# Recurrent attention and a routed expert layer on one core: state sums before routing, an earlier and smaller first list, one gather of late rows, index lists on VectorE

## The chip, the core and the metric

The kernel runs on one core of a Trainium2 chip. The metric is the time of one execution on the device, in microseconds (us); the kernel before was timed in 3 runs. One further execution was recorded by the hardware profiler, and all rows of a trace come from such an execution. Engine names: PE is TensorE's matmul, PEld its weight load, DVE is VectorE, ACT is ScalarE, POOL is GpSimd, SP is the engine that issues most transfers. Each engine works through its own instructions strictly in order and waits on the others by semaphores.

## The reference

```python
for t in range(S):                       # attention: 4 batches, 8 heads, 768 steps, width 40
    m_new = np.maximum(f_gate[:, :, t] + m, i_gate[:, :, t])
    f_stab = np.exp(f_gate[:, :, t] + m - m_new)
    i_stab = np.exp(i_gate[:, :, t] - m_new)
    C = f_stab * C + i_stab * outer(v_t, k_t)
    n = f_stab * n + i_stab * k_t
    y_t = sigmoid(o_t) * (C @ q_t) / max(abs(n . q_t), 1)
x = y as 3072 rows of 320
g_idx, g_w = argmax and softmax weight of x @ w_group            # 4 groups
e_idx, e_w = argmax and softmax weight of x @ w_expert[g_idx]    # 4 experts in each
out[row] = g_w * e_w * (relu(x[row] @ w1[g, e]) @ w2[g, e])      # 320 -> 1024 -> 320
```

Each of the 3072 rows goes to one of 16 experts. With the inputs of this case the fullest expert has 321 rows in the end, 267 after five of the six time chunks and 222 after four (counted with the reference).

## The kernel before

**Attention.** The 768 steps are cut into 6 chunks of 128, and a chunk of one batch is a unit: 24 units, number 4c + b, worked off in order of time by `unit(u)` (L958 to L1001) and, from unit 20 on, by the hand-written `last_units` (L1028 to L1144). All instructions are issued in the order in which this Python code calls them. For one unit PE does the scores (L199, tile `sp`), the products with the values (L281, `acc`), the new state (L248, `st`), the product with the state of earlier chunks (L229, `acc` of the next unit) and the transposes of the finished rows (L319, `tp`). POOL multiplies the state by its decay (L255, `Cflat`), the rows by their denominators (L301, `x`) and cuts the mask triangle (L158, `ab`); ACT takes the exponentials (L190). DVE forms the denominators and gated rows (L286 to L296), scales `acc` (L238), multiplies scores by the mask (L204, `pt`, two instructions) and adds the new state (L266, two instructions). `st` and the two `acc` banks have one buffer each, so a unit's state product waits until the state sum of the unit before has read `st`.

**Routing.** When four units of a chunk are done, `chunk_logits` (L348) and the generator `route` (L364) find each row's expert and its place in that expert's list, in 18 short steps that `go_on` deals out over the next units: six ahead of `scores` in three of four units (L959, L970). `mark` (L481) then builds one-hot matrices, and PE adds them to the lists (L501, `listed` L505).

**First expert.** After three chunks `first_experts` (L550) chooses the expert with most rows. Its list is drawn by `select` (L509) in `last_units` when five chunks are listed (L1102); up to 256 rows are gathered early, and the first layer runs after the last unit in `early_expert` (L707, PE L720 first layer, L735 to L737 second). The rows of that expert which come later are collected by another way: `late_marks` and `late_rows` (L522, L529) multiply the rows of the last units, still in SBUF, by selection matrices on PE, and `late_gather` (L1013) fetches the rest. They run as a second narrow pass of the same expert, `expert((0, 1), ...)` (L1336).

**All experts.** `expert` (L857) runs experts 1 to 15 one after the other, first layer at L780, second at L825 to L833; number r has CAPS[r] slots, so 6 and 7 have the same width (224), as have 11 to 14 (160). From number 6 on they are narrow: DVE adds two halves (`hs`, L888) before each relu. Weights are split into a high and a low part, by ACT (L750) and DVE (L754). At the start of expert r, `load_ix(r + 2)` (L665) draws the list of expert r + 2 with `select` on POOL: a product `lsel` on POOL (L511), its sum `lsum` on DVE (L513), two index writes on POOL (L519, L520). POOL also issues all gathers (L636) and scatters (L640), and after some experts waits until its scatters have drained (L849).

```python
        select(r, top[:, r, :] if r < NPICK else rt["sel"][:, r, :], nc.gpsimd)
...
        ahead, behind = STEPS.get(u) or ((6, 0), (2, 0), (6, 0), (6, 1))[u % B]
...
        go_on(ahead)
```

Of the kernel before, what the change touches and what calls it, by code (L numbers as in the profile page):

```python
# [18 lines left out]
P = 128  # L19
# [25 lines left out]
SIDE = (B, B, B, B, B - 1)  # L45
# [4 lines left out]
HAND = 20  # L50
# [12 lines left out]
def lstm_moe(ctx: ExitStack, tc: tile.TileContext, gates, qkT, nat, wcat, w1, w2, cst, out):  # L63
# [7 lines left out]
    peek = dram.tile([1, 2], F32, name="peek")  # L71
# [22 lines left out]
    late_f = const.tile([P, NEARLY], F32, name="late_f")  # L94
# [24 lines left out]
    abs_ = [ap_.tile([P, H, P], F32, name=f"ab{i}") for i in range(4)]  # L119
    nts = [ap_.tile([P, NTW + DM + WIN], F32, name=f"nt{i}") for i in range(4)]  # L120
    ps_s = att.enter_context(tc.tile_pool(name="ps_s", bufs=3, space=PSUM))
# [177 lines left out]
    def rows(u, e=None):  # L299
        x = wk.tile([P, ROW], F32, name="x", bufs=3) if u < HAND else mxp.tile([P, ROW], F32, name="xg", bufs=8)  # L300
        (e or nc.gpsimd).tensor_tensor(x[:, 0:DM].rearrange("p (h d) -> p h d", d=D), st_[u]["sr"],  # L301
                                       bc(st_[u]["den"].unsqueeze(2), (P, H, D)), op=ALU.mult)
        st_[u]["x"] = x

    def store_rows(u):
# [4 lines left out]
        if c == NCH - 1:  # L310
            no_order("early", ins, "store")
# [27 lines left out]
    def logits(u):  # L339
        c, b = divmod(u, B)  # L340
        if c < NCH - 1 and b < SIDE[c]:
            return chunk_logits(SIDE[c]) if b == SIDE[c] - 1 else None
        if b == 0:
            rt["bank"] = ps_1.tile([P, LG + B * 20], F32, name="lg")
        for k, (x, w) in enumerate(terms(b)):
            mm(rt["bank"][:, LG + b * 20:LG + (b + 1) * 20], x, w[:, 0:20], start=(k == 0), stop=(k == 2))

    def chunk_logits(n):  # L348
        bank = rt["bank"] = ps_1.tile([P, LT + P], F32, name="lg")
        for k in range(3):  # L350
            for b in range(n):
                x, w = terms(b)[k]
                mm(bank[32 * b:32 * (b + 1), LT - P:LT], w, x, start=(k == 0), stop=(k == 2))
        nc.scalar.copy(lgT[0:32 * n, :], bank[0:32 * n, LT - P:LT])

    def turned_logits(c):
        bank, n = rt["bank"], SIDE[c]
        lv = bank[:, LT:LT + 32 * n]
        nc.tensor.transpose(out=lv, in_=lgT[0:32 * n, :], identity=ident[0:32 * n, 0:32 * n])
        return route(c, 0, n, bank, lv.rearrange("p (b e) -> p b e", e=32)[:, :, 0:20], n < B)  # L360
# [3 lines left out]
    def route(c, b0, b1, bank, lv=None, ahead=False):  # L364

        n = b1 - b0
        cur, nxt = ohsum[rt.setdefault("n", 0) % 2], ohsum[(rt["n"] + 1) % 2]
        rt["n"] += 1
        if lv is None:
            lv = bank[:, LG + b0 * 20:LG + b1 * 20].rearrange("p (b e) -> p b e", e=20)  # L370
# [27 lines left out]
        def sums():  # L398
            ohs = post.tile([P, NE], BF16, name="ohs")
            with nc.allow_low_precision("whole numbers up to 4"):  # L400
                nc.vector.tensor_reduce(ohs, oh.rearrange("p b e -> p e b"), axis=AX.X, op=ALU.add)
            nc.vector.tensor_tensor(nxt, cur, ohs, op=ALU.add)

        if ahead:
            sums()
        rk = bank[:, b0 * NE:b1 * NE].rearrange("p (b e) -> p b e", b=n)
# [5 lines left out]
        if b1 == B:  # L412
            cnt = bank[:, B * NE:B * NE + NE]
            mm(cnt, ones_b, cur, start=True, stop=False)
            for b in range(n):
                mm(cnt, ones_b, oh[:, b, :], start=False, stop=(b == n - 1))
        yield
        if b1 == B:
# [1060 lines left out]
```

## Time and profile before

| | us |
|---|---|
| median of 3 runs | 452.38 |
| lowest and highest run | 449.66, 454.95 |
| the profiled execution, its own time | 456.12 |
| span of its trace, first to last instruction | 454.5 |
| PE busy | 406.7 (89%) |
| DVE busy | 336.9 (74%) |
| ACT busy | 261.7 (58%) |
| POOL busy | 186.1 (41%) |
| mean granted PE clock | 0.939 of full speed |

The span starts and ends with the first and last instruction; 1.6 us of the execution lie around it. A busy share is a mean over stages with different limits: an engine at 74% can be what everyone waits for in one stage and idle in another.

### The profile page before, as it was taken

To read this page: it belongs to the slowest core of one execution; us is meant where nothing else is said; L and a number is where in the kernel's file an instruction comes from. 1 tells how busy PE (TensorE), PEld (TensorE's weight loads), DVE (VectorE), ACT (ScalarE), POOL (GpSimd) and SP (SyncE) were. 2 spreads that over 40 slices of the span, in tenths; PEclk is the share of its full clock that TensorE was granted. 3 is DMA by queue.
4 is the path that set the end of the run, shared out by engine and by line. 5 is a ranking of instruction groups with operands and counts; after the bars stand their busy time and mean duration, and the time that the engine had idled before them with its cause. 6 is when DMAs were issued, how large, how long until landed. Compare 5 with 4: busy or idle time off the path is not lost.

```text
span 454.5 us, 9459 instructions
## 1 busy us (share of the span) xinstructions
PE 406.7 (89%) x3369; PEld 377.9 (83%) x3369; DVE 336.9 (74%) x841; ACT 261.7 (58%) x621; POOL 186.1 (41%) x227
## 2 busy tenths in 40 slices
PE   8799779687877986789999999999799999998995
PEld 5688768577867775789999999999799998897994
DVE  5776685777676997768576756676688997997993
ACT  3486464555543643404455646656567886886783
POOL 6576346354544111106363152452343334664221
PEclk9889898989988999569999999999899999999899
DMA  6999878776765742701758465756466777776400
GB/s 183 310 304 303 260 213 265 218 220 210 205 207 181 262 181 61 274 17 43 272 195 321 162 205 170 259 187 234 178 211 222 239 257 266 241 260 265 149 16 11
DMA packets 22469, 93.59 MB, mean 206 GB/s; under 512 B 3746, under 2 KB 7801, under 8 KB 18836
## 3 DMA queue, kind: packets, MB, share of 16 engines
q1 hardware_dynamic: 18180, 78.64, 52.3%
q0 software_dynamic: 3920, 13.95, 9.2%
q8 instruction: 28, 0.46, 0.4%
q10 hardware_dynamic: 320, 0.37, 0.4%
q14 instruction: 21, 0.17, 0.2%
HBM read 83.41 MB, written 10.23 MB: 206 GB/s over the span
## 4 chain that ended last, share of the span: by engine, by line
PE 51%; issue 18%; DVE 13%; POOL 10%; ACT 4%; DMA 1%; POOLq 1%; SPq 0%; ACTq 0%; DVEq 0%
PE psh L780 13%; PE acc L229 5%; POOL out_dram L640 4%; PE po L825 4%; PE po L826 4%; PE po L827 4%; PE acc L281 3%; DVE pt L204 2%; PE sp L199 2%; PE psh L720 2%; PE tp L319 2%; PE st L248 2%; POOL ab L158 2%; PE psh L800 2%; POOL xg L636 2%
## 5 line engine op out<-in xcount | busy, mean ns | idle before, releaser
L780 PE MATMUL psh<-xhl,w1h 128*128 128x320 f32 (+4 forms) x336 | 87.7, 322 | 5.7 <-DVE hs L888 5.5
L640 POOL DMA_INDIRECT out_dram<-y,ix x34 | 43.3, 1275 | 108.8 <-ACT y L839 86.7
L780 PEld LDWEIGHTS psh<-xhl,w1h 128*128 128x128 f32 x336 | 57.4, 190 | 7.5 <-DVE hs L888 6.5
L825 PE MATMUL po<-w2h,hh 128*128 128x320 f32 (+1 forms) x184 | 58.5, 318 | 0.0
L754 DVE TENSOR_TENSOR w2l<-w2s,w2h 128x640 fp32r<-128x640 f32 x64 | 53.0, 845 | 6.0 <-ACT w2h L750 5.3
L826 PE MATMUL po<-w2l,hh 128*128 128x320 f32 (+1 forms) x184 | 57.0, 310 | 0.0
L827 PE MATMUL po<-w2h,hh 128*128 128x320 f32 (+1 forms) x184 | 56.9, 309 | 0.0
L190 ACT ACTIVATE ab<-ab,bcol 128x128 f32<-128x128 f32 x176 | 53.8, 389 | 4.3 <-POOL ab L158 3.8
L281 PE MATMUL acc<-nt,pt 128*128 128x128 f32 (+1 forms) x384 | 49.7, 283 | 5.6 <-ACT nt L155 3.2
L281 PEld LDWEIGHTS acc<-nt,pt 128*128 128x128 f32 x384 | 46.2, 196 | 9.0 <-ACT nt L155 3.4
L636 POOL DMA_INDIRECT xg<-x_d,ix x34 | 38.5, 1133 | 29.4 <-DVE lf L1023 15.4
L780 PE MATMUL psh<-xhl,w1l 128*128 128x160 f32 (+6 forms) x256 | 49.0, 273 | 0.0
L780 PE MATMUL psh<-xhl,wsk 128*128 128x320 f32 (+4 forms) x168 | 46.5, 315 | 0.9 <-DVE wsk L754 0.9
L750 ACT CAST w2h<-w2s 128x640 fp32r<-128x640 f32 x64 | 44.8, 723 | 0.0
L780 PEld LDWEIGHTS psh<-xhl,w1l 128*128 128x128 f32 x256 | 43.8, 190 | 0.5
L321 ACT COPY xT<-tp 128x256 f32<-128x256 f32 x24 | 8.9, 372 | 58.5 <-PE tp L319 34.2
L754 DVE TENSOR_TENSOR w1l<-w1s,w1h 128x1024 fp32r<-128x1024 f32 x32 | 38.9, 1220 | 3.7 <-ACT w1h L750 3.6
L204 DVE TENSOR_TENSOR pt<-sp,ab 128x512 f32<-128x512 f32 x48 | 31.1, 684 | 10.0 <-PE sp L199 8.5
L825 PEld LDWEIGHTS po<-w2h,hh 128*128 128x128 f32 (+1 forms) x184 | 34.4, 187 | 0.6
L826 PEld LDWEIGHTS po<-w2l,hh 128*128 128x128 f32 (+1 forms) x184 | 34.3, 186 | 0.0
L827 PEld LDWEIGHTS po<-w2h,hh 128*128 128x128 f32 (+1 forms) x184 | 34.2, 186 | 0.0
L750 ACT CAST w1h<-w1s 128x1024 fp32r<-128x1024 f32 x32 | 33.5, 1049 | 0.0
(221 smaller groups left out, 908.3 us busy)
## 6 DMA issues: line engine op xcount, KB each, us to landing
w1s<-in_w_dram SPq DMA_DIRECT2D x12, 1536.0 KB
w2s<-in_w_dram SPq DMA_DIRECT2D x13, 1280.0 KB
nt<-in_nat_dram SPq DMA_DIRECT2D x24, 484.0 KB
ab<-a_d SPq DMA_DIRECT2D x22, 512.0 KB
qk<-in_qkT_dram SPq DMA_DIRECT2D x48, 160.0 KB
x_d<-x SPq DMA_DIRECT2D x20, 192.0 KB
w1s<-in_w_dram SPq DMA_DIRECT2D x4, 768.0 KB
w1s<-in_w_dram POOLq DMA_DIRECT2D x2, 1536.0 KB, 7.3
```

The source lines that it names most:

```text
L190: nc.scalar.activation(ab[:, j, :], ab[:, j, :], AF.Exp, bias=bcol[:, c, b * H + j:b * H + j + 1])
L204: nc.vector.tensor_tensor(pt, t["pm"][hh], t["ab"][:, 4 * hh:4 * hh + 4, :], op=ALU.mult)
L229: mm(acc[:, 2 * pr:2 * pr + 2, 0:CW], t["qk"][:, 1, pr, :], Cflat[:, o:o + 2 * CW].rearrange("p (r e) -> p r e", r=2), start=(pr == 0), st ...
L281: mm(o, t["pm"][j % 2][:, j // 2, :], v, start=(c == 0 and n == 0), stop=(n == H - 1), skip_group_check=True)
L636: return nc.gpsimd.indirect_dma_start(out=o, out_offset=None, in_=src, in_offset=bass.IndirectOffsetOnAxis(ap=idx, axis=0))
L640: return nc.gpsimd.indirect_dma_start(out=out, out_offset=bass.IndirectOffsetOnAxis(ap=idx, axis=0), in_=y, in_offset=None, bounds_check=N ...
L750: nc.scalar.copy(t[names[0]][:, dst], src[r][:, s])
L754: nc.vector.tensor_tensor(o, src[r][rows, s], h.bitcast(F32), op=ALU.subtract)
L780: mm(ps[:, g, 0:n_], w[:, s], x, start=(n == 0), stop=(n == len(todo) - 1))
L825: mm(po[0:m], hh[:, f, t], w2h[:, s], start=st0, stop=False)
L826: mm(po[0:m], hh[:, f, t], w2l[:, s], start=False, stop=False)
L827: mm(po[0:m], hh[:, f, tl], w2h[:, s], start=False, stop=sp0)
```

## The change

Six things move. (1) In `unit`, the state sum (`state2`) comes before the masks, and the routing steps are dealt two by two: ahead of the scaling of `acc`, ahead of the masks, behind them. (2) Units 20 and 21 go through `unit` like the others; the four units of a chunk are always routed together. (3) The first expert's list is drawn in unit 21 from four chunks (16 units) in place of five; expert 0's weights are split in units 21 to 23, with the low parts on POOL. (4) The eight steps of its first layer are dealt among the last transposes, logits and routing; the second layer among the last lists. (5) The selection products of late rows go; when the lists are complete one gather, on POOL, fetches all late rows. (6) `select` runs on DVE alone, and the lists of experts 3 to 15 are drawn at the start of experts 1 to 7, two at a time from number 2.

```diff
     def unit(u):
-        ahead, behind = STEPS.get(u) or ((6, 0), (2, 0), (6, 0), (6, 1))[u % B]
+        one, two, three = STEPS.get(u) or ((2, 2, 1), (0, 0, 0), (2, 2, 2), (2, 2, 2))[u % B]
...
+        go_on(one)
         run(carried2, u)
         listed()
-        go_on(ahead)
         scores(u + 1)
...
         values(u)
+        run(state2, u)
+        go_on(two)
+        if u == NU - 3:
+            rt["early"] = select(top[:, 0, :], nc.vector)
+            xgs[0] = load_x(EARLY, rt["early"], True)
         masked(u + 1, 0)
         masked(u + 1, 1)
         store_rows(u - 1)
-        run(state2, u)
...
-        go_on(behind)
+        go_on(three)
...
+def early_first(W, ws):          # the loop of early_expert, one step f a yield
+        for f in range(NF):
...
+            if g:
+                relu(ps, f - 1)
+            yield
...
-    def casts(r):
+    def casts(r, e=None):
...
-                nc.vector.tensor_tensor(o, src[r][rows, s], h.bitcast(F32), op=ALU.subtract)
+                (e or nc.vector).tensor_tensor(o, src[r][rows, s], h.bitcast(F32), op=ALU.subtract)
...
-        select(r, top[:, r, :] if r < NPICK else rt["sel"][:, r, :], nc.gpsimd)
+        ixs[r] = select(top[:, r, :] if r < NPICK else rt["sel"][:, r, :], nc.vector)
...
+    def all_lists():
+        listed()
+        late_gather(picked(top[:, 0, :], nc.vector))
+        load_ix(1)
+        xgs[1] = load_x(CAPS[1], ixs[1])
...
+        norm1(d)
+        norm2(d)
+        gated(d)
+        rows(d, nc.vector)
...
+        first = early_first(EARLY, wsp_[0])
+        steps(first, 2)
+        do(early_loads)
+        store_rows(d)
+        turn_rows(d)
+        split(w2_splits, 2)
+        go_on(9)
+        mark(2, nc.vector)
+        do(lows, 1)
+        mark(2, nc.vector)
+        steps(first)
+        logits()
+        steps(first)
+        last = turned_logits(NCH - 1)
+        listing(ps_1.tile([P, 4, P], F32, name="tp", tag="tp"))
+        steps(last, 6)
+        listed()
+        do(lows, 1)
+        steps(first, 2)
+        steps(last)
+        split(w2_splits, 2)
+        steps(first, 2)
+        steps(last, 12)
...
+        second = early_second(EARLY, wsp_[0], rt["early"])
+        for act, _ in own:
+            act()
+        steps(second, 6)
+        listing(ps_1.tile([P, 4, P], F32, name="tp", tag="tp"))
+        steps(second, 3)
+        all_lists()
+        next(experts)
+        load_e(2, [ET.SP, ET.Pool])
+        steps(second, 8)
+        xl = early_turn((0, 1), LATE, xgs["late"], ((ps_1, "av"),))
+        do(xl)
...
-        expert((0, 1), LATE, rt["late"], [], (), lambda: turn2(1, CAPS[1], xgs[1]))
+        expert((0, 1), LATE, rt["late"], [(lambda: None, low) for _, low in own], (), lambda: turn2(1, CAPS[1], xgs[1]))
...
-                load_ix(r + 2)
+                while len(ixs) < min(NE - 1, 2 * r + 1):
+                    load_ix(len(ixs) + 1)
```

How the instructions move. First DVE in unit 14, the first unit after a chunk's logits, before the change (`acc` is scaled, `lists` takes up finished list parts, `mx` to `oh` are routing steps, `pt` the masks, `Cflat` the state sum; `sr`, `den` belong to the unit before):

```order
L296 SCALAR_TENSOR_TENSOR sr<-nt_111,acc 128x320
L238 TENSOR_TENSOR acc<-acc,eacol 128x8x41
L507 TENSOR_TENSOR lists<-lists,tp 128x96
L374 TENSOR_REDUCE mx<-lg 128x20
L377 TENSOR_TENSOR df<-lg,mx 128x80
L384 SCALAR_TENSOR_TENSOR eq<-df,cs 128x80
L387 TENSOR_REDUCE m_1526<-eq 128x20
L390 TENSOR_TENSOR oh_1528<-eq,m_1526 128x80
L394 TENSOR_TENSOR oh<-oh_1528 128x64
L204 TENSOR_TENSOR pt<-sp,ab_109 128x512 x2
L266 TENSOR_TENSOR Cflat<-Cflat,st 40x4x41 x2
L286 TENSOR_SCALAR den<-acc 128x8
```

and the same unit after it:

```order
L294 SCALAR_TENSOR_TENSOR sr<-nt_112,acc 128x320
L361 TENSOR_REDUCE mx<-lg 128x20
L364 TENSOR_TENSOR df<-lg,mx 128x80
L236 TENSOR_TENSOR acc<-acc,eacol 128x8x41
L486 TENSOR_TENSOR lists<-lists,tp 128x96
L264 TENSOR_TENSOR Cflat<-Cflat,st 40x4x41 x2
L371 SCALAR_TENSOR_TENSOR eq<-df,cs 128x80
L374 TENSOR_REDUCE m_1560<-eq 128x20
L202 TENSOR_TENSOR pt<-sp,ab_110 128x512 x2
L377 TENSOR_TENSOR oh_1583<-eq,m_1560 128x80
L381 TENSOR_TENSOR oh<-oh_1583 128x64
```

The state sum stood behind six routing steps and two masks; now two steps, the scaling and the list stand ahead of it, and the masks behind it.

Second PE, from unit 23's transposes on (before), with `tp` for transposes of finished rows and for shift products, `tpm` for the gathered rows, `lg` for logits and ranks, `late` for the selection of late rows, `psh` for the first layer of the first expert:

```order
L319 MATMUL tp<-cs,xg 128x128 x2
L319 MATMUL tp<-cs,xg 64x128
L1010 MATMUL tp<-lsum,shift 128x2 x3
L697 MATMUL tpm<-cs,xg 128x128 x6
L346 MATMUL lg<-wc,xT 128x20 x3
L532 MATMUL late<-latem,xg 128x128 x3
L533 MATMUL late<-iw,latem 128x2
L407 LDWEIGHTS lt_b
L407 MATMUL lg<-oh,lt_b 128x32
L409 LDWEIGHTS ones_b
L409 MATMUL lg<-oh,ones_b 128x16
```

and after the change, from unit 23's values (`acc`) on:

```order
L279 MATMUL acc<-nt_114,pt 128x128 x7
L279 MATMUL acc<-nt_114,pt 128x64
L317 MATMUL tp<-cs,x 128x128 x2
L317 MATMUL tp<-cs,x 64x128
L685 MATMUL psh<-xhl,w1h 128x256 x4
L685 MATMUL psh<-xhl,wsk 128x256 x2
L685 MATMUL psh<-xhl,w1l 128x256 x2
L685 MATMUL psh<-xhl,w1h 128x256 x4
L685 MATMUL psh<-xhl,wsk 128x256 x2
L685 MATMUL psh<-xhl,w1l 128x256 x2
L317 MATMUL tp<-cs,x 128x128 x2
L317 MATMUL tp<-cs,x 64x128
```

Before, 21 rows with shift products, logits, selection products and ranks stand between unit 23's transposes (L339) and the first `psh`; now `psh` begins behind the transposes of unit 22 and ahead of those of unit 23, and the selection products are gone.

Third the start of experts 4 and 5 on POOL, before (`out_dram` are scatters of results, `xg` gathers of rows, `lsel` and `ix` the list):

```order
L640 DMA out_dram<-y,ix 3072x320 x3
L511 TENSOR_TENSOR lsel<-lists,sel 128x96
L519 TENSOR_SCALAR ix<-lsum 128x3
L520 COPY ix<-lsum 128x3
L636 DMA xg<-x_d,ix 128x384
L636 DMA xg<-x_d,ix 96x384
L640 DMA out_dram<-y,ix 3072x320 x3
L511 TENSOR_TENSOR lsel<-lists,sel 128x96
L519 TENSOR_SCALAR ix<-lsum 128x3
L520 COPY ix<-lsum 128x3
L636 DMA xg<-x_d,ix 128x384
L636 DMA xg<-x_d,ix 96x384
```

and after:

```order
L598 DMA out_dram<-y,ix 3072x320 x3
L594 DMA xg<-x_d,ix 128x384
L594 DMA xg<-x_d,ix 96x384
L598 DMA out_dram<-y,ix 3072x320 x3
L594 DMA xg<-x_d,ix 128x384
L594 DMA xg<-x_d,ix 96x384
```

and on DVE at the start of expert 2 after the change (`y` ends the expert before, `hh` is the first relu of this one):

```order
L805 TENSOR_TENSOR y<-y,po 64x320
L490 TENSOR_TENSOR lsel<-lists,sel 128x96
L492 TENSOR_REDUCE lsum<-lsel 128x6
L501 TENSOR_SCALAR ix<-lsum 128x3
L502 COPY ix<-lsum 128x3
L490 TENSOR_TENSOR lsel<-lists,sel 128x96
L492 TENSOR_REDUCE lsum<-lsel 128x6
L501 TENSOR_SCALAR ix<-lsum 128x3
L502 COPY ix<-lsum 128x3
L840 SCALAR_TENSOR_TENSOR hh<-psh,hh 128x2x256
L840 SCALAR_TENSOR_TENSOR hh<-psh,hh 128x2x64
```

POOL only issues transfers there; DVE does all four instructions of a list, of two lists in a row, where it did one sum that waited for POOL.

## Rows read from the trace of the kernel before

**Rows 1.** windows: us; PE, PEld, DVE, ACT, POOL busy; clock, DMA share, GB/s

```profile
34.90:149.80 114.90, 95.65 (x1108) 85.98 (x1105) 82.45 (x248) 60.12 (x214) 55.27 (x82) 0.91 0.75 228
149.80:177.40 27.60, 22.64 (x217) 19.80 (x216) 24.20 (x109) 11.85 (x38) 5.34 (x6) 1.00 0.49 172
177.40:199.10 21.70, 15.96 (x84) 14.78 (x84) 17.36 (x79) 6.85 (x16) 1.75 (x1) 0.57 0.47 170
199.10:216.30 17.20, 17.16 (x126) 16.61 (x124) 12.62 (x28) 5.78 (x9) 7.41 (x7) 0.95 0.11 30
...
315.10:440.20 125.10, 118.94 (x789) 112.51 (x789) 104.39 (x189) 94.58 (x172) 50.56 (x57) 0.97 0.62 216
```

**Rows 2.** PE's L229: count, duration min/median/max in ns, first and last start in us

```profile
L229 PE MATMUL acc<-Cflat,qk x160: 275/275/557, 34.9 to 171.3; 128*128 128x112 f32 x160
```

**Rows 3.** chain that ended last, units 13 and 14: start, us, what

```profile
98.79 1.07 PE acc L229 x8
...
104.58 1.07 PE acc L229 x8
...
112.33 1.98 PE acc L229 x8
```

**Rows 4.** timeline of unit 14: start, us, engine, operation [idle before, releaser]

```profile
105.73 0.75 POOL L255 TENSOR_TENSOR Cflat<-Cflat,dec 128x328 f32<-128x328 f32 x1 [1.13 <-PE acc L229]
...
107.81 1.09 POOL L158 TENSOR_SCALAR_AFFINE_SELECT ab<-ab 128x1024 f32<-128x1024 f32 x1
...
107.82 1.17 DVE L384 SCALAR_TENSOR_TENSOR eq<-df,cs 128x80 f32<-128x80 f32 x1
...
109.03 0.24 DVE L387 TENSOR_REDUCE m<-eq 128x20 f32<-128x80 f32 x1
...
110.92 0.65 DVE L266 TENSOR_TENSOR Cflat<-Cflat,st 40x164 f32<-40x164 f32 x2
...
111.83 0.51 PE L248 MATMUL st<-nt,kw 128*40 128x41 f32 x16 [2.30 <-DVE den L286]
```

**Rows 5.** timeline of PE, last values

```profile
175.45 2.00 PE L281 MATMUL acc<-nt,pt 128*128 128x128 f32 x16 [2.38 <-DVE acc L238]
```

**Rows 6.** timeline from there on, PE and DVE

```profile
194.94 1.22 PE L720 MATMUL psh<-xhl,w1h 128*128 128x256 f32 x4 [2.64 <-DVE xhl L700]
...
199.39 0.69 DVE L725 SCALAR_TENSOR_TENSOR hh<-psh,hh 128x512 fp32r<-128x512 f32 x1 [0.35 <-ACT hh L724]
...
202.05 1.11 PE L501 MATMUL tp<-mark 128*128 128x96 f32 x8
```

**Rows 7.** timeline of PE, first product of the late pass

```profile
216.27 0.39 PE L780 MATMUL psh<-xhl,w1h 128*128 128x256 f32 x1
```

**Rows 8.** waits from 225 us on: in total, times, longest

```profile
DVE lsum L513 <- POOL lsel L511: 19.8, 7, 6.8
...
PE psh L780 <- DVE hs L888: 5.5, 3, 2.6
```

**Rows 9.** timeline of PE, first products of experts 6, 7, 8, 13, 14, 15

```profile
315.07 0.36 PE L780 MATMUL psh<-xhl,w1h 128*128 128x448 f32 x1
...
333.84 0.37 PE L780 MATMUL psh<-xhl,w1h 128*128 128x448 f32 x1
...
348.29 0.34 PE L780 MATMUL psh<-xhl,w1h 128*128 128x384 f32 x1
...
412.91 0.31 PE L780 MATMUL psh<-xhl,w1h 128*128 128x320 f32 x1
...
428.74 0.31 PE L780 MATMUL psh<-xhl,w1h 128*128 128x320 f32 x1
...
440.19 0.28 PE L780 MATMUL psh<-xhl,w1h 128*128 128x256 f32 x1
```

**Rows 10.** transfers issued, the late gather: KB each, us to landing

```profile
xg<-x_d,li POOLq DMA_INDIRECT x1, 4.7
```

**Rows 11.** page, costliest groups: DVE's low part of a weight

```profile
L754 DVE TENSOR_TENSOR w1l<-w1s,w1h 128x1024 fp32r<-128x1024 f32 x32 | 38.9, 1220 | 3.7 <-ACT w1h L750 3.6
```

More of the change, by code (lines that the diff above doesn't have):

```diff
@@ L396, in route @@
         yield
[L398 to L406, printed above, removed]
+        rk = bank[:, 0:n * NE].rearrange("p (b e) -> p b e", b=n)
         mm(rk, lt_b, oh, start=True, stop=False)
@@ L452, in route @@
         yield
-        if not ahead:
-            sums()
+        ohs = post.tile([P, NE], BF16, name="ohs")
+        with nc.allow_low_precision("whole numbers up to 4"):
+            nc.vector.tensor_reduce(ohs, oh.rearrange("p b e -> p e b"), axis=AX.X, op=ALU.add)
+        nc.vector.tensor_tensor(nxt, cur, ohs, op=ALU.add)
     def go_on(n=1):
@@ L570, in first_experts @@
             early_loads.extend(load_tasks(r, 2))
-        for act, low in sum(casts(0), []):
-            early_splits.append(lambda act=act, low=low: (act(), lows.append(low)))
+        for tasks in casts(0, nc.gpsimd):
+            early_splits.append(tasks)
         yield
@@ L956, in aside, with split @@
             n -= 1
+    def split(tasks, n=1):
+        for _ in range(n):
+            act, low = tasks.pop(0)
+            act()
+            low()
     def unit(u):
-        ahead, behind = STEPS.get(u) or ((6, 0), (2, 0), (6, 0), (6, 1))[u % B]
+        one, two, three = STEPS.get(u) or ((2, 2, 1), (0, 0, 0), (2, 2, 2), (2, 2, 2))[u % B]
         run(load_ab, u + 4)
-        load_qk(u + 3)
+        run(load_qk, u + 3)
         norm1(u - 1)
@@ L994, in unit @@
         turn_rows(u - 1)
-        if u == HAND - 1:
-            logits(u - 1)
-        if u % B < 2:
+        if u % B < 2 and u > B or u == 19:
             mark()
-        if u == 16:
+        if u == 19:
+            mark()
+        if u == min(ASIDE):
             asides.append(first_experts())
-        aside(4)
+        aside(ASIDE.get(u, 0))
+        if u in (NU - 5, NU - 4):
+            do(early_loads, 2)
+        if u == NU - 3:
+            split(early_splits[0])
     def steps(g, n=1):
@@ L1005, in steps, with late_gather @@
             next(g, None)
[L1007 to L1008 removed]
+    def late_gather(f):
+        tp = ps_1.tile([P, 2], F32, name="tp", tag="tp")
         for k in range(NB):
[L1010 to L1019 removed]
@@ L1108, in last_units @@
         gated(c)
+        go_on(3)
         carried2(d)
-        rows(c, nc.vector)
+        rows(c)
         values(d)
-        logits(b)
-        r3 = route(NCH - 1, 0, 2, rt["bank"])
-        steps(r3, 6)
-        steps(early_counts(), 9)
-        do(early_splits, 1)
-        steps(r3)
-        turn(c)
-        busy(1)
-        steps(r3)
+        do(xl)
+        go_on(4)
+        store_rows(c)
+        turn_rows(c)
+        score_banks.close()
+        pools["ps_h"] = early_banks.enter_context(tc.tile_pool(name="ps_h", bufs=3, space=PSUM, side="right"))
         norm1(d)
@@ L1279, in lstm_moe @@
         pools["xhl"] = [mxp]
-        for u in range(5, HAND):
+        early_banks = ExitStack()
+        for u in range(5, NU - 2):
             if u == 5:
```

326 lines of the change are left out of this document (95 added, 231 removed).

## Prediction, made before the changed kernel was run

> **What bounds the kernel now.** I read the windows by stage first, since a mean over the span hides that each stage has its own limit. From 34.9 to 149.8 us, units 4 to 19, no engine is full: PE is busy 95.65 of 114.9 us, DVE 82.45, POOL 55.27, and the granted clock is 0.91 of full [rows 1]. L229 has 160 products, eight a unit, first at 34.9 us [rows 2]; so this stage has 16 units of 114.9 / 16 = 7.18 us, of which PE is busy 5.98, DVE 5.15, POOL 3.45. The reader is to see that these units wait for one another rather than for an engine.
>
> The chain and the timeline say how. Unit 13 lies between two `acc` products at 98.79 and 104.58: 5.79 us [rows 3], with no routing dealt into it. Unit 14 lasts from 104.58 to 112.33, 7.75 us. There PE stands 2.30 us before its state product `st` at 111.83 [rows 4], which needs the one `st` buffer, and that is read by the state sum L266 at 110.92, 0.65 us, the last but for two masks and six routing steps on DVE. After the stand the next `acc` takes 1.98 us in place of 1.07 [rows 3]: PE came back at the lower of its two levels, 1.2 GHz.
>
> After the last values (175.45 + 2.00) comes a worse stage: from 177.4 to 199.1 us PE has 0.57 of its clock, and DVE works 17.36 of 21.7 us [rows 1, 5]. The first layer of the first expert begins only at 194.94 [rows 6], the late pass at 216.27 [rows 7].
>
> The experts after that keep PE full, with exceptions. DVE waits 19.8 us in seven places for POOL's `lsel`, up to 6.8 at once, and PE 5.5 us in three places, up to 2.6, for DVE's `hs` [rows 8]. Experts of one width show what that costs: number 6 takes 333.84 - 315.07 = 18.77 us, number 7 14.45; number 13 takes 15.83, number 14 11.45 [rows 9].
>
> **The change part by part.** All sums are against the profiled execution, 456.12 us; the median of the runs shown is 452.38, 3.7 lower.
>
> *State sum first, routing in twos (units 4 to 19).* Nothing is added; the order changes. The state sum will stand behind two steps, the `acc` scaling and perhaps a list, and needs POOL's decay product, which starts as soon as `acc` is done and takes 0.75 [rows 4]. 0.75 and 0.65 for the sum, with an estimated 1 for a list between them, is 2.4 us from the end of `acc`; PE meanwhile has transposes and scores and then the values, which alone take 2.00 [rows 5], so it no longer stands at `st`. What is late next is either PE itself or DVE, whose 5.15 us a unit stay. From below the period is bounded by PE's 5.98 us with the slow clock taken out, about 5.5 (5.98 x 0.91); unit 13 ran at 5.79 with the logits in it; from above by today's 7.18, or more if a new wait comes. I take 6.0, near unit 13, since PE and DVE, both over 85% busy then, still wait for each other in order. Gain 16 x 1.18 = **18.9 us** (0 to 27). Faster units ask more of the DMAs: 0.75 of their time x 7.18 / 6.0 = 0.90; loads are issued three to four units ahead, so I cost this at nothing; if that cover is gone it is part of the upper bound.
>
> *Units 20 to 23.* They take 27.6 us from the first `acc` to the last values, 24.20 of it DVE [rows 1]. The routing of chunk 4 is no longer cut in three and one, and moves partly behind the values; the early list, the shift matrices and eight of the routing steps stay. I take 5.3 + 5.5 for units 20 and 21, 4.5 to the end of unit 22's values, and 6.7 more for unit 23, whose `acc` scaling stands on DVE behind the shift matrices: 22.0. Gain **5.6 us** (0 to 8).
>
> *From the last values to the late pass.* Before: 216.27 - 177.45 = 38.8 us. After, PE has less to do than that: the first layer is 64 products and the second 48, most of the 17.16 us of PE in 199.1 to 216.3 [rows 1], so about 20 us with transposes, logits and lists. But the lists now end it. DVE's work from here to the last mask is today's 17.36, less three low parts at 1.22 = 3.7 that go to POOL [rows 1, 11], plus four relu low parts at 0.69 = 2.8 [rows 6]; the late masks that go and the rest of chunk 4 that comes I set equal: 16.5 us. Then the four list products on PE, 1.1 [rows 6], and some six short steps for list, choice, shift and index, 2; then the gather on POOL, behind the scatter of the first results, 1 more, and 4.7 to landing, what today's late gather takes [rows 10]; then transposes, high and low part, 1.5. Sum 16.5 + 1.1 + 2 + 1 + 4.7 + 1.5 = 26.8. PE has run dry by then for some 5 us, and as in unit 14 it will start again at the lower level; I add 1.5. The late pass starts 28.3 us after the last values: gain **10.5 us** (2 to 14).
>
> *Low parts on POOL.* Seven subtractions. POOL's 328 columns took 0.75 us [rows 4], so 1024 take about 2.3 and 640 about 1.5 us: 3 x 2.3 + 4 x 1.5 = 12.9 us in all, from below DVE's 1.22 for 1024 [rows 11]. POOL has little else from 149.8 on, 5.34 of 27.6 us, and 1.75 of 21.7 [rows 1]. I cost this at nothing: the first three lie beside units 22 and 23, the rest ends before the second layer needs it. But unit 14 warns: DVE's `eq`, 1.17 us, began 0.01 after POOL's `ab` cut of 1.09 and ended when that ended, where its like `m` took 0.24 [rows 4]. The Trainium skill, "SBUF — State Buffer", section "Who interferes with whom", says that a VectorE instruction with two SBUF inputs and a GpSimd one that reads SBUF exclude each other for the whole instruction. The row agrees. By that rule each of the four last subtractions may hold DVE once. In time of this kernel that is up to 4 x 1.5 = 6 us more on DVE's path to the last mask; it is a rival below.
>
> *Lists on DVE, two at a time.* DVE gets four instructions of about a quarter us a list, in place of one: 13 lists, 0.6 each, inside experts 1 to 7, where PE's next tiles cover it. What goes is the wait for POOL, which sits behind scatters and their drains: expert 6 gains 18.77 - 14.45 = 4.3, expert 13 15.83 - 11.45 = 4.4, of which I take 4.0, since both neighbours' work lies between such starts; for PE's third wait I take 1.0 (the two shorter ones hold 5.5 - 2.6 = 2.9): 9.3. The late pass takes three low parts of expert 1 with it, 3.7 us of DVE beside 9.4 us of PE; I take 0.7 lost. Gain **8.6 us** (0 to 10).
>
> Sum: 18.9 + 5.6 + 10.5 + 8.6 = 43.6, so 456.1 - 43.6 = 412.5 on the profiled execution's footing and 408.8 on the median's. I forecast 411.
>
> **The rivals.** *DVE becomes the bound of the units.* For it: 5.15 us of work plus the waits for `acc`, lists and POOL in a strict order. Against: unit 13. At 6.7 us the first term is 7.7 in place of 18.9: 422.
>
> *The lists end later.* The port of rows 4 and the exposed gather: 6 us by the subtractions and 2 more of low clock, 411 + 8 = 419. For it: everything from the last logits to the late pass is one chain through DVE, PE, POOL and a transfer. Against: only some DVE steps have two inputs in SBUF.
>
> *The experts gain nothing.* The list work on DVE, or gathers that now wait in another place, keeps the experts' gaps: 411 + 8.6 = 420. For it: DVE is busy 104.39 of 125.1 us there [rows 1]. Against: the lists are done by expert 7, and expert 13 has none.
>
> *Slower than before: the state sum ties DVE to POOL.* In order, masks now wait for the state sum, and that for POOL's decay product. If POOL's whole queue of a unit, 3.45 us, came into the loop on top of unit 13's 5.79, a unit would take 9.24, 16 x 2.06 = 33 us more than today, and 411 + 18.9 + 33 = 463. It decides from the point at which the units' loss eats the 24.7 us gained elsewhere, 7.18 + 24.7 / 16 = 8.7 us a unit. Against: the decay product stands first in POOL's queue after `acc`, with 1.13 us idle before it in unit 14 [rows 4].
>
> **How the numbers follow.** The forecast 0.58; DVE-bound units 0.18; later lists 0.11; experts gain nothing 0.07; slower 0.04; something between, near no change, 0.02. The range: units at 5.6 and full gain behind give some 398; DVE-bound units together with later lists 430, and a little beyond for both and the experts. So 397 to 434. A measurement of this kernel tells about 1% from no change; faster by more than that 0.93, within it 0.03, slower 0.04.
>
> **What would show it.** In the profile after: `acc` products of units 4 to 19 some 6 us apart, with no stand of PE before `st`; the last values near 153 us; the first layer right behind them, at full clock; PE idle for 4 to 6 us before the late pass, at about 181; no wait of DVE for a list from expert 1 on, experts 6 and 13 as long as 7 and 14. It would be wrong if units stayed near 7 us, if PE's clock stayed low behind the last values, or if DVE stood for several us beside POOL's subtractions.

## The result, and the profile after

The changed kernel takes 408.06 us (median of 4 runs, 406.27 to 410.32), 0.902 of the time before (95% interval 0.895 to 0.909). In a later series the same kernel took 407.08 (6 runs, 403.39 to 409.58). The profiled execution took 410.32 us, its span is 408.6 in place of 454.5, and the mean granted clock 0.974 in place of 0.939.

The windows by stage answer to [rows 1]: us; PE, PEld, DVE, ACT, POOL busy; granted clock, DMA share, GB/s. The first row is units 4 to 19, the second units 20 to 23 up to the end of the last values, the third and fourth from there to the late pass, the last experts 6 to 14.

```profile
34.20:122.40 88.20, 86.40 (x1108) 77.89 (x1105) 78.44 (x262) 59.96 (x215) 55.72 (x83) 1.00 0.91 291
122.40:148.50 26.10, 20.85 (x210) 19.13 (x210) 20.60 (x64) 13.45 (x41) 14.50 (x14) 0.93 0.78 269
148.50:160.00 11.50, 9.37 (x90) 8.59 (x89) 9.85 (x30) 4.27 (x11) 3.23 (x2) 0.93 0.43 148
160.00:178.50 18.50, 14.63 (x93) 13.45 (x92) 11.68 (x44) 6.79 (x10) 7.96 (x7) 0.86 0.14 40
...
277.10:394.00 116.90, 116.90 (x803) 112.19 (x802) 108.33 (x199) 94.74 (x173) 39.36 (x34) 1.00 0.65 233
```

The 16 units lasted 114.9 us and now last 88.2: 5.51 us each. PE works 86.40 of them at full clock: this stage is now bounded by PE. In the next three rows PE is idle for part of the time again, and the mean clock is 0.86 to 0.93; from 277.1 us on PE is busy throughout, at 1.00.

Unit 16 of after in the timeline (start, us, engine, operation [idle before, releaser]) answers to [rows 4]:

```profile
100.88 0.75 POOL L253 TENSOR_TENSOR Cflat<-Cflat,dec 128x328 f32<-128x328 f32 x1 [2.50 <-DMA qk<-in_qkT_dram]
...
102.05 0.50 DVE L236 TENSOR_TENSOR acc<-acc,eacol 128x328 f32<-128x328 f32 x1
102.45 0.65 DVE L264 TENSOR_TENSOR Cflat<-Cflat,st 40x164 f32<-40x164 f32 x2
102.60 2.00 PE L279 MATMUL acc<-nt,pt 128*128 128x128 f32 x16 [0.39 <-DVE acc L236]
...
104.53 0.51 PE L246 MATMUL st<-nt,kw 128*40 128x41 f32 x16
...
104.82 1.29 DVE L202 TENSOR_TENSOR pt<-sp,ab 128x512 f32<-128x512 f32 x2
```

The state sum (L264) follows the `acc` scaling at once and is over at 103.1, while PE is still at its values. The state product `st` at 104.53 waits for nothing; in unit 14 of before it stood 2.30 us. From 34.2 to 122.4 us no `st` of after waits at all.

From 122 to 180 us the waits of PE include these (total us, times, longest):

```profile
PE acc L279 <- DVE acc L236: 4.4, 2, 2.9
...
PE tp L480 <- DVE mark L473: 3.0, 2, 2.1
...
PE psh L743 <- issue: 1.2, 1, 1.2
...
PE tpm L655 <- DMA xg<-x_d,li: 0.9, 1, 0.9
```

Ahead of both large ones DVE has long instructions beside POOL's subtractions of low parts (L717). In the timelines of DVE, POOL and PE:

```profile
137.48 2.35 POOL L717 TENSOR_TENSOR w1l<-w1s,w1h 128x1024 fp32r<-128x1024 f32 x1 [2.40 <-ACT w1h L713]
138.28 1.66 DVE L377 TENSOR_TENSOR oh<-eq,m 128x80 f32<-128x80 f32 x1
139.97 0.63 DVE L381 TENSOR_TENSOR oh<-oh 128x64 bf16<-128x64 f32 x1
...
143.35 1.21 DVE L403 TENSOR_SCALAR sm<-sm 128x20 f32<-128x20 f32 x1
144.47 0.49 DVE L236 TENSOR_TENSOR acc<-acc,eacol 128x328 f32<-128x328 f32 x1
...
145.02 3.50 PE L279 MATMUL acc<-nt,pt 128*128 128x128 f32 x16 [2.89 <-DVE acc L236]
...
151.43 0.41 DVE L467 TENSOR_TENSOR mark<-irow,lo__70 128x256 f32<-128x256 f32 x1
...
152.92 3.23 POOL L717 TENSOR_TENSOR w2l<-w2s,w2h 128x640 fp32r<-128x640 f32 x2 [5.17 <-ACT w2h L713]
153.00 1.76 DVE L467 TENSOR_TENSOR mark<-irow,lo__70 128x256 f32<-128x256 f32 x1
154.69 1.58 DVE L470 TENSOR_TENSOR mark<-irow,hi__71 128x96 f32<-128x96 f32 x1
156.30 0.43 DVE L473 TENSOR_TENSOR mark<-mark,iw 128x96 f32<-128x96 f32 x2
...
163.04 1.50 DVE L423 TENSOR_SCALAR slot<-slot 128x4 int32<-128x4 int32 x1
```

A mark takes 0.41 us alone (151.43) and 1.76 beside POOL's subtraction. Counted so, `oh`, `sm`, `sg`, `mark` and `slot` took 8.2 us more than elsewhere in the same trace. Of these, 7.8 us lie beside POOL's seven subtractions; the other 0.4, in the second `oh` at 139.97, lies beside another POOL instruction, the row product `x` (L299) of 139.80 to 140.51.

First products of experts 6, 7, 8 and 13, 14, 15 answer to [rows 9] (duration min/median/max in ns, first and last start):

```profile
L743 PE MATMUL psh<-xhl,w1h x1: 367/367/367, 279.7 to 279.7; 128*128 128x448 f32 x1
L743 PE MATMUL psh<-xhl,w1h x1: 363/363/363, 294.1 to 294.1; 128*128 128x448 f32 x1
L743 PE MATMUL psh<-xhl,w1h x1: 338/338/338, 308.7 to 308.7; 128*128 128x384 f32 x1
...
L743 PE MATMUL psh<-xhl,w1h x1: 308/308/308, 371.0 to 371.0; 128*128 128x320 f32 x1
L743 PE MATMUL psh<-xhl,w1h x1: 310/310/310, 383.0 to 383.0; 128*128 128x320 f32 x1
L743 PE MATMUL psh<-xhl,w1h x1: 280/280/280, 394.5 to 394.5; 128*128 128x256 f32 x1
```

Expert 6 takes 14.4 us (18.77 before), expert 7 14.6; expert 13 12.0 (15.83), expert 14 11.5.

### The profile page after: what moved, and what is told of

Same layout as the page of the kernel before. It is cut to its first block, busy times and chain, and to the rows that moved or that the text cites. A ratio compares the mean times of both kernels' runs of the same rounds, so it can differ in the third digit from the quotient of the medians.

```text
span 408.6 us, 9340 instructions
## 1 busy us (share of the span) xinstructions
PE 382.6 (94%) x3335; PEld 358.5 (88%) x3335; DVE 329.6 (81%) x818; ACT 260.1 (64%) x620; POOL 177.0 (43%) x197
## 4 chain that ended last, share of the span: by engine, by line
PE 67%; DVE 10%; issue 9%; ACT 4%; DMA 4%; POOL 3%; another core or an unknown queue 1%; POOLq 1%; SPq 0%; DVEq 0%
PE psh L743 21%; PE acc L279 7%; PE po L788 6%; PE po L789 5%; PE po L790 5%; PE sp L197 3%; PE acc L227 3%; PE po L794 2%; ACT ab L188 2%; DMA x_d<-x 2%; PE po L793 2%; PE psh L763 2%; PE st L246 2%; PE tp L317 1%; POOL out_dram L598 1%
## 5 line engine op out<-in xcount | busy, mean ns | idle before, releaser
L717 DVE TENSOR_TENSOR w2l<-w2s,w2h 128x640 fp32r<-128x640 f32 x60 | 48.6, 825 | 6.1 <-ACT w2h L713 5.1
L594 POOL DMA_INDIRECT xg<-x_d,ix x34 | 35.2, 1036 | 19.8 <-PE psh L743 9.8
L717 DVE TENSOR_TENSOR w1l<-w1s,w1h 128x1024 fp32r<-128x1024 f32 x30 | 36.6, 1220 | 3.8 <-ACT w1h L713 3.6
L789 PEld LDWEIGHTS po<-w2l,hh 128*128 128x128 f32 (+1 forms) x184 | 34.2, 186 | 0.0
L850 ACT COPY hs<-psh 128x320 f32<-128x320 f32 (+3 forms) x44 | 19.6, 447 | 22.6 <-PE psh L743 16.1
```

The source lines that it names most:

```text
L594: return nc.gpsimd.indirect_dma_start(out=o, out_offset=None, in_=src, in_offset=bass.IndirectOffsetOnAxis(ap=idx, axis=0))
L717: (e or nc.vector).tensor_tensor(o, src[r][rows, s], h.bitcast(F32), op=ALU.subtract)
L789: mm(po[0:m], hh[:, f, t], w2l[:, s], start=False, stop=False)
L850: nc.scalar.copy(src[p], ps[:, :, W:2 * W])
```

## The experiments

All of them change the kernel after. Their spans fall into the same five stages, cut where the first products of units 4 and 20 begin (L227), where the last values end and where the late pass begins:

| us, profiled execution | to unit 4 | units 4-19 | 20 to last values | to late pass | rest | span |
|---|---|---|---|---|---|---|
| before | 34.9 | 114.9 | 27.6 | 38.8 | 238.2 | 454.5 |
| after | 34.2 | 88.2 | 26.1 | 30.0 | 230.1 | 408.6 |
| after, recorded again | 35.0 | 88.1 | 26.2 | 28.1 | 228.1 | 405.5 |
| state sum behind masks | 34.8 | 101.0 | 27.9 | 30.8 | 228.2 | 422.7 |
| routing in one piece | 35.3 | 101.4 | 28.9 | 27.8 | 230.6 | 424.0 |
| both | 34.0 | 118.0 | 30.4 | 30.9 | 228.2 | 441.5 |
| lists on POOL | 33.7 | 88.2 | 26.0 | 30.0 | 237.5 | 415.4 |
| low parts on DVE | 33.6 | 88.3 | 30.5 | 35.3 | 228.2 | 415.9 |
| counts in unit 19 | 32.5 | 88.2 | 25.4 | 33.9 | 228.1 | 408.1 |
| counts in gaps | 34.5 | 88.3 | 22.0 | 31.0 | 230.4 | 406.2 |
| low parts in gaps | 34.3 | 88.2 | 29.2 | 24.5 | 228.0 | 404.2 |
| gather ahead | 33.6 | 88.2 | 26.0 | 30.4 | 228.3 | 406.5 |
| all in gaps | 32.4 | 88.2 | 24.5 | 24.1 | 228.1 | 397.3 |
| moved earlier still | 33.9 | 88.2 | 22.5 | 29.3 | 228.1 | 402.0 |

Where the edit leaves the units alone, units 4 to 19 repeat to 0.1 us, so a stage tells more than a median; the start (32.4 to 35.3) varies from one execution to the next.

### The kernel after, again

> The kernel after, unchanged, once more beside the three others, so that differences of one per cent can be read: 406 to 410 us by its first four runs. All theories expect the same.

407.08 us. Two stages differ from the first recording, which the last section takes up.

### State sum and dealing, each undone and both

The state sum behind the masks:

```diff
         values(u)
-        run(state2, u)
         go_on(two)
...
         store_rows(u - 1)
+        run(state2, u)
```

> The kernel after, with the state sum again behind the two masks; the routing stays dealt in small pieces. Theory (sum and dealing each matter, and the loss of before came from both in a row): a unit goes from 5.51 to about 5.8 us, what unit 13 of before took with its sum behind the masks and no routing: 16 units give 5 us, 411 to 415 us. Rival B (the dealing alone made the gain): 408 us. Rival C (the place of the sum alone made it): units of 7.2 us again, 432 to 436 us.

The routing in one piece:

```diff
-        go_on(one)
         run(carried2, u)
         listed()
+        go_on(one + two + three)
...
-        go_on(two)
...
-        go_on(three)
```

> The kernel after, with the routing again in one piece behind the acc scaling and ahead of the state sum and the masks, up to six steps at once; the state sum stays ahead of the masks. Theory (both matter): three units of four get some 1.5 us of routing ahead of sum and masks, of which about half shows on TensorE: 416 us (411 to 421). Rival B (the dealing alone made the gain of the units): 432 to 436 us. Rival C (the place of the sum alone made it): 408 to 410 us.

Both edits together:

> The kernel after, with both undone: the routing in one piece of up to six steps, and the state sum behind it and behind the masks. All theories: the units go back towards 7.18 us with TensorE standing some 2 us before its state product: 16 x 1.6 = 25 us more, 430 to 436 us. If it stays under 420, the gain of the units comes from something else, such as the routing of the last chunk that is no longer cut or the marks.

Measured: 422.98 (419.1 to 426.35), 424.32 (421.42 to 425.95) and 443.56 us (439.89 to 446.47). Units 4 to 19 lose 12.8, 13.2 and 29.8 us against after. The windows of units 4 to 19 in the three, in this order:

```profile
34.80:135.80 101.00, 89.70 (x1106) 80.87 (x1105) 79.67 (x257) 59.62 (x214) 55.28 (x82) 0.97 0.85 255
```

```profile
35.30:136.70 101.40, 89.14 (x1106) 80.72 (x1105) 83.47 (x256) 60.20 (x215) 55.58 (x83) 0.97 0.87 260
```

```profile
34.00:152.00 118.00, 97.28 (x1110) 87.63 (x1105) 83.59 (x252) 60.01 (x214) 55.33 (x82) 0.90 0.73 222
```

Rivals B and C both fall: neither edit alone keeps the gain or loses all of it, and the two add to 26.0 of the 29.8 us. All three medians lie above the theory's ranges. For the sum its size was too small (5 us). For the dealing its 8 us were near: of the 13.2, 5.2 are unit 18 alone, 11.46 us in place of 6.31. There the edit puts ten steps in one piece, where the kernel before had six, and PE stands 2.92 us ahead of the rank products. That part does not undo the change but is worse than before, so the pieces of before cost some 8.0 us.

PE's largest waits between 35 and 122 us of the span (total us, times, longest), first before, then after, then the sum behind the masks, the routing in one piece, and both:

```profile
PE st L248 <- DVE den L286: 5.0, 3, 2.3
PE st L248 <- DVE Cflat L266: 3.6, 2, 2.4
...
PE acc L279 <- DVE acc L236: 1.5, 3, 0.5
...
PE st L246 <- DVE Cflat L264: 7.7, 5, 2.2
...
PE st L246 <- DMA qk<-in_qkT_dram: 5.3, 4, 1.8
PE st L246 <- DVE Cflat L264: 4.0, 4, 1.1
...
PE st L246 <- DVE den L284: 8.8, 4, 2.3
```

So the stand ahead of `st`, gone in after, returns with each edit. Where a transfer or `den` is named as the releaser, the state sum ended just before: with the routing in one piece it ended at 114.04, and `st` began at 114.29 after 1.77 us of standing. With the sum behind the masks:

```profile
75.00 0.65 DVE L264 TENSOR_TENSOR Cflat<-Cflat,st 40x164 f32<-40x164 f32 x2
...
75.91 0.51 PE L246 MATMUL st<-nt,kw 128*40 128x41 f32 x16 [0.72 <-DVE Cflat L264]
```

Unit 13 of before, from which I took 5.8 us, had no routing at all in it; with the small pieces that are dealt now, a sum behind the masks is already too late for PE. With both edits PE is back at a clock of 0.90, and the units take 7.38 us, near the 7.18 of before. Most of the 3.1 us by which the 16 are longer lies in unit 13 (7.36 us for 5.79) and in units 18 and 19 together (15.50 for 14.32), of which 18 carries ten steps in one piece.

### The lists on POOL again

```diff
-        ixs[r] = select(top[:, r, :] if r < NPICK else rt["sel"][:, r, :], nc.vector)
+        ixs[r] = select(top[:, r, :] if r < NPICK else rt["sel"][:, r, :], nc.gpsimd)
...
-                while len(ixs) < min(NE - 1, 2 * r + 1):
-                    load_ix(len(ixs) + 1)
+                load_ix(r + 2)
```

> The kernel after, with the lists of experts 3 to 7 chosen on GpSimd again, one per expert, as before. Theory (the experts gained because VectorE no longer waits for GpSimd's list behind its scatters): waits of VectorE's lsum for GpSimd's lsel come back, 10 to 20 us in all, of which TensorE shows about what the experts gained, 8.1 us: 415 to 418 us. Rival (the experts gained by earlier gathers or by the first expert's low parts that moved): no such waits on TensorE's path, 407 to 410 us.

416.98 us (415.09 to 418.55), as the theory has it. The waits of before [rows 8] are back, and only the last stage changes, by 7.4 to 9.4 us against the two recordings of after:

```profile
DVE lsum L492 <- POOL lsel L490: 20.6, 8, 6.8
```

The edit undoes the engine and the drawing two at a time together; which of the two matters was not separated.

### The low parts on DVE, at the same places

```diff
-        for tasks in casts(0, nc.gpsimd):
+        for tasks in casts(0):
```

> The kernel after, with the seven low parts of the first expert's weights on VectorE instead of GpSimd. Theory (a VectorE instruction that runs beside one of these GpSimd subtractions is held until it ends): in the trace after, oh, sm and sg between 137 and 147 us and mark and slot between 153 and 165 us took 8.2 us more than their usual durations (oh 1.66 for 0.24 and 0.63 for 0.24, sm 1.21 for 0.17, sg 0.88 for 0.17, mark 1.76 for 0.42 and 1.58 for 0.25, slot 0.83 and 1.50 for 0.17). These go, and the subtractions themselves come, three of 1.22 and four of an estimated 0.8, 6.9 us: 404 to 410 us, and no mark, oh or sm above 0.7. Rival (GpSimd's subtractions cost VectorE nothing, and those instructions were long for another reason): they stay long and 6.9 us come on top: 413 to 416 us.

415.97 us (411.95 to 419.01): the theory's 404 to 410 is missed, and the time is the rival's, but not for its reason. In the timeline of DVE the marks are short again, and something else is there:

```profile
136.92 1.23 DVE L717 TENSOR_TENSOR w1l<-w1s,w1h 128x1024 fp32r<-128x1024 f32 x1 [3.84 <-ACT w1h L713]
...
157.56 1.56 DVE L717 TENSOR_TENSOR w2l<-w2s,w2h 128x640 fp32r<-128x640 f32 x2 [3.60 <-ACT w2h L713]
...
161.99 0.41 DVE L467 TENSOR_TENSOR mark<-irow,lo__70 128x256 f32<-128x256 f32 x1
162.32 0.25 DVE L470 TENSOR_TENSOR mark<-irow,hi__71 128x96 f32<-128x96 f32 x1
...
169.01 1.56 DVE L717 TENSOR_TENSOR w2l<-w2s,w2h 128x640 fp32r<-128x640 f32 x2 [3.70 <-ACT w2h L713]
```

So POOL's subtractions did hold DVE. But a low part that follows right behind its cast makes DVE wait for ACT, three times, 11.1 us in all, and everything in DVE's queue waits with it. On POOL the waits for the same casts (up to 5.17 us above) did not show on PE.

### The counts of the first expert elsewhere

First, meant for the ends of units 19 and 20, they all came to stand at the end of 19:

```diff
-        steps(early_counts(), 9)
...
-    ASIDE = {15: 3, 16: 4, 17: 12}
+    ASIDE = {15: 3, 16: 4, 17: 12, 19: 4, 20: 9}
...
+        if u == 19:
+            asides.append(early_counts())
```

> The kernel after, with the counts and shift matrices of the first expert (L541 to L553) dealt to the ends of units 19 and 20 instead of standing in one piece in unit 22 ahead of the acc scaling of unit 23. Theory: TensorE's stand of 2.89 us before the last values came from 1.7 us of these instructions and from sm held beside GpSimd's subtraction; without them the scaling comes 1.7 us earlier: 405.5 to 407 us. Rival A (the subtractions then hold VectorE in another place, and the last values come no earlier): 408 us. Rival B (the clock counts too: without the stand the last values run at full clock, 2.0 for 3.5 us): 403 to 405 us.

Then in two waits of DVE, with a `yield` ahead of the shift matrices:

```diff
-        steps(early_counts(), 9)
...
-    ASIDE = {15: 3, 16: 4, 17: 12}
+    ASIDE = {15: 3, 16: 4, 17: 12, 20: 4}
...
+        if u == NU - 4:
+            asides.append(early_counts())
...
         run(carried2, u)
+        if u == NU - 3:
+            aside(9)
         listed()
```

> The kernel after, with the counts of the first expert in two of VectorE's own waits: L541 to L549 at the end of unit 20 (0.96 us idle there), the shift matrices behind the acc scaling of unit 21 (1.37 us idle). Theory (the counts cost 2.9 us of TensorE in unit 22 only because they stood ahead of an acc scaling; at the end of unit 19, behind two pairs of marks, they did the same, unit 20 took 9.2 in place of 5.9): units 20 and 21 stay at 5.9 and 6.1 us, the last values begin 2 to 3 us earlier: 404.5 to 406.5 us. Rival (POOL's subtractions hold VectorE as long in another place, and it is these that count): 407 to 409 us.

413.69 (409.66 to 414.36) and 408.12 us (405.07 to 409.62). The first is slower than after, and slower than its theory and both rivals had it; the second gains nothing, the rival's time. In the first, behind two pairs of marks, they make PE wait 3.3 us for the `acc` scaling of unit 20 (the unit takes 9.2 us for 5.9). Its recording in the table is the fastest of its six runs, so the table shows less than the loss. In the gaps, the stand before the last values does go, and the stage takes 22.0 us instead of 26.1 and 26.2. But the two stages together take 53.0 us, against 56.1 and 54.3 in the recordings of after, and the median does not move. PE and POOL there:

```profile
145.00 2.34 POOL L718 TENSOR_TENSOR wsk<-w1s,wsk 64x1024 fp32r<-64x1024 f32 x1
147.42 0.72 POOL L299 TENSOR_TENSOR x<-sr,den 128x320 f32<-128x320 f32 x1
...
148.20 0.90 PE L317 MATMUL tp<-cs,x 128*128 128x128 f32 x3 [3.44 <-POOL x L299]
```

The rows of unit 22 (L299) are formed on POOL, behind two subtractions of 2.35 us. Where PE does not wait for DVE it now waits 3.44 us for them: a second wait stood hidden behind the first, since in after these rows are ready no earlier (147.75 us, here 148.14). The kernel with the counts in unit 19 has the same wait of 3.4 us. A hold moves too, as the rival said: in the gaps `sm` takes 0.18 us for 1.21, but `sg`, now beside a subtraction for longer, 1.86 for 0.88.

### The low parts on DVE, where its casts are long done

On top of the kernel with the counts in unit 19; `cast_only` issues the casts and puts the low parts into `wlows` (the comments are added here):

```diff
+        cast_only(w1_splits, 2)      # in unit 22, ahead of the masks
...
+        do(wlows, 2)                 # unit 22, behind oh
+        cast_only(w2_splits, 2)
...
+        do(wlows, 3)                 # unit 23, ahead of its norm
...
+        cast_only(w2_splits, 2)
         last = turned_logits(NCH - 1)
...
         steps(last)
+        do(wlows, 2)                 # where DVE waited for the rank products
```

> As the kernel with the counts dealt early, and all seven low parts of the first expert on VectorE, but each at a place where its cast is long done: the casts are issued ahead of their places, three low parts of w1 in units 22 and 23, two of w2 ahead of the last norm, two where VectorE waited 1.50 us for the rank products. Theory (GpSimd's subtractions held VectorE for 8.2 us in all, and on VectorE the same work cost 416 us above only because it waited 3.6 and 3.7 us for casts just issued): no long oh, sm, mark or slot, no wait for a cast, the way from the last values to the late pass 2 to 4 us shorter: 400 to 404 us. Rival (VectorE's own 6.9 us of subtractions eat what the holds gave, as the 416 us suggest): 406 to 412 us.

405.66 us (403.54 to 406.83), 8.0 less than the kernel that it was built on, though it carries the 3.3 us of the counts in unit 19. From the last values to the late pass it takes 24.5 us instead of 28.1 to 30.0 in after. That is 3.6 to 5.5 us, no mark or slot is long, and no low part waits for a cast, as the theory has it; only one `sm` still takes 0.72 us, beside POOL's row product `x` of 0.72. The total lies above the theory's range and below the rival's, and the stage ahead, which has the counts of unit 19 and the low parts of w1 on DVE, is 3 us longer than in after. The two stages follow:

```profile
122.50:151.70 29.20, 23.63 (x210) 22.03 (x209) 22.23 (x68) 14.67 (x43) 7.46 (x11) 0.82 0.75 256
151.70:176.20 24.50, 20.88 (x179) 18.94 (x177) 19.00 (x78) 9.79 (x19) 4.81 (x5) 1.00 0.23 81
```

### The late gather two steps earlier

```diff
-        steps(second, 3)
+        steps(second, 1)
         all_lists()
...
-        steps(second, 8)
+        steps(second, 10)
```

> The kernel after, with one step of the second layer instead of three between the last list products and the late list (two more follow behind it), so that the late gather also stands ahead of the scatter of the first block on GpSimd. Theory (the late pass waits for this gather): the index comes some 1 us earlier and the gather another 1.0 us, of which TensorE can show at most the 0.87 and 1.16 us for which it stood before the late pass: 406 to 407.5 us. Rival (TensorE's own products fill that time, and the stands are the chain of transposes and low part): 408 us, nothing.

406.14 us (403.24 to 409.58), not to be told from 407.08. The wait for the gather goes, but PE is idle for as long as before in this stage (6.1 us, against 6.0 and 7.0), which takes 30.4 us at a clock of 0.88: inconclusive in time.

### All of it, and more

`gaps_all` puts the last three together: counts in gaps, low parts in gaps, gather ahead.

> The last kernel, with the low parts on VectorE in its gaps and with the late gather two steps earlier. Theory (the way from unit 22 to the late pass is VectorE's work, and these are separate pieces of it): against the kernel with the low parts in gaps (405.66 us), unit 20 gives back 3.3 us and what follows at the lower clock another 1: 400 to 402.5 us. Rival (VectorE's total from unit 20 on sets the end wherever its pieces stand): 404 to 406 us.

401.81 us (398.94 to 402.67), in the theory's range and below the rival's: 0.893 of the time before (0.888 to 0.899), where the kernel after, in the same series, has 0.904 (0.896 to 0.911). Every run of it was below every run of after. Its two stages:

```profile
120.60:145.10 24.50, 20.70 (x211) 19.14 (x210) 22.33 (x68) 14.64 (x43) 7.47 (x11) 0.94 0.88 303
145.10:169.20 24.10, 21.15 (x179) 19.16 (x177) 19.09 (x78) 9.62 (x19) 3.83 (x4) 0.99 0.23 79
```

The counts in gaps showed nothing in the median alone, and the low parts on DVE cost 8 us at the wrong places; here the two stages take 48.6 us together, against 56.1 and 54.3, and PE no longer waits for POOL's `x`. What each of the three edits gives here was not separated. Then more was moved out of units 22 and 23, the comments added here:

```diff
-        if u in (NU - 5, NU - 4):
+        if u in (NU - 6, NU - 5):
             do(early_loads, 2)
+        if u == NU - 4:
+            cast_only(early_splits[0], 2)
...
+        if u == NU - 3:
+            do(wlows, 1)             # twice: behind the acc scaling, and at the end
...
+        carried2(d)                  # ahead of the norm of unit 22
         norm1(c)
```

> As the last, with more moved out of the full stretch of VectorE (139 to 167 us): the weights of the first expert loaded one unit earlier, two low parts of w1 (1.22 us each) in the waits of unit 21, the third in unit 22, the shift matrices behind the last mark, and the acc scaling of unit 23 ahead of the norm of unit 22. Theory (VectorE is full from unit 22 to the last mark, so work taken out shows in full): 2.4 us of low parts and 0.7 of shift matrices less, and no stand before the last values: 397 to 400 us. Rival A (loads that come a unit earlier stand in the queue ahead of a unit's own, the DMAs being 0.91 busy): units 19 to 21 each lose 1 us or more, 401 to 405 us. Rival B (TensorE, not VectorE, sets the end there): as the last.

402.18 us (399.0 to 403.6), no better: rival B's number, though its reason is not shown. The loads do not disturb the units (88.2), so rival A falls. The last values come 2 us earlier and the next stage, at a clock of 0.88, takes 5.2 more. One of the two low parts of unit 21 waited 2.42 us for its cast again. How much each of the two took was not separated.

## Why the prediction was right, point by point

The time was right, 411 forecast against 408.06, and so was its sum, 43.6 us of gain against 45.9 between the spans. Some of its steps were not: the units gave 7.8 us more than forecast, units 20 to 23 gave 4.1 less, and a term put at nothing was not nothing. That these nearly cancel in the sum is luck; the order of the parts and the mechanism of the largest are not.

*Units 4 to 19: 18.9 us predicted, 26.7 measured.* The step that failed is "I take 6.0, near unit 13, since PE and DVE, both over 85% busy then, still wait for each other in order". They hardly do: with sum and steps where they stand now PE works 86.40 of 88.20 us and waits 1.5 us for DVE, and the lower bound of the prediction, 5.5 us a unit, is what came. Unit 13 was the wrong model: it had the sum still behind the masks, and undoing that alone costs 12.8 us. The mechanism, the stand before `st`, is shown by the three experiments: the stands return with either edit, and the clock falls to 0.97 with one and 0.90 with both. The cover for the transfers held at a DMA share of 0.91. The rivals of DVE-bound units and of a state sum tied to POOL did not come; nor did the slower outcome.

*Units 20 to 23: 5.6 predicted, 1.5 measured.* The step is "6.7 more for unit 23, whose `acc` scaling stands on DVE behind the shift matrices". The cost was named and too small: from the end of unit 22's values (138.9) to the last values it took 9.6 us. DVE had `oh` and `sm` held beside POOL's subtractions in the same stretch, PE stood 2.9 us, and the last values took 3.50 us at the lower clock in place of 2.00. With the counts elsewhere the stage takes 22.0, the number predicted, but the prediction had them in it.

*From the last values to the late pass: 28.3 us predicted, 30.0 and 28.1 measured.* The size was right by terms that were not, which is luck again. DVE's way to the last mark took 20.0 us (148.5 to 168.5) and not 16.5; from there it took 10.0 and not the 11.8 of list products, steps, gather, landing, turn and low clock. Of the 20.0 us DVE was busy for 17.4, with 4.7 of that held in `mark` and `slot`: its own work, some 12.8 us, was less than the 16.5.

*Low parts on POOL: nothing predicted, 8.2 us of held instructions measured.* "I cost this at nothing" failed, and one of the prediction's own signs of being wrong came, DVE held for several us beside POOL's subtractions. What the rival "the lists end later" said of them came in part, 4.7 us of holds on the way to the last mark for its 6; its 8 us of time did not (30.0 and 28.1 for 28.3), as DVE's own work was less. The row of before that warned, `eq` at 1.17 us [rows 4], was right: in unit 22 of after, with no such neighbour, `eq` takes 0.24. The Trainium skill, "SBUF — State Buffer", section "Who interferes with whom", names casts and operations with a scalar, too, among those that can contend with GpSimd; the trace agrees: L403 took 1.21 us for 0.17 and L423 1.50 for 0.17. It exempts reductions, and L401 beside the same subtraction as L403 took its usual 0.23. On DVE, at the same places, the same work cost 8 us more still; where each cast was done in time the low parts no longer cost that.

*Experts: 8.6 predicted, 8.1 and 10.1 measured.* Experts 6 and 13 came down to their neighbours, and PE is busy 116.90 of 116.90 us from 277.1 on. The lists account for nearly all of it: with them on POOL, one an expert, the last stage takes 237.5 us, before it took 238.2.

## What to carry to other kernels

Work that is moved to an idle engine is not free when that engine shares something with the one that sets the end: look in the trace for short instructions that are long beside it. When one wait ends a stage, look what ends second, since removing one of two may show nothing: moving the counts did not, while POOL's subtractions still kept PE waiting for the rows behind them. In an engine that works in order, an instruction belongs where its input is long ready, not behind the one that makes it.

## What the runs showed of the hardware that was not expected

The same code ran at two clocks behind stands of like length (PE idle for 6.0 and 7.0 us in the stage ahead). The late pass, first recording of after and then the second:

```profile
178.50:189.50 11.00, 10.99 (x73) 10.75 (x74) 8.04 (x17) 3.88 (x11) 2.18 (x3) 0.84 0.77 284
```

```profile
177.40:187.00 9.60, 9.60 (x74) 9.24 (x74) 7.80 (x17) 3.93 (x11) 2.18 (x3) 1.00 0.83 297
```

Part of the first stretch ran at the lower level, 1.2 GHz, the second wholly at 2.4. The stage before it took 30.0 us at 0.89 and 28.1 at 1.00. In all recordings that stage had PE idle for some us, and its clock lay between 0.73 and 1.00. What decides this was not found; together it moves a single time by 3.9 us (1.9 and 2.0), as much as the smaller experiments here, and is why they are read by stages.
